# Pooled attention: normalizing by a diagonal in the transposing product, a byte activation for the first weights, paced staging

## The chip, the core and the metric

One core of one Trainium2 chip runs the whole program. The metric is the device time of one execution, in microseconds (us). Five engines work from queues of their own: TensorE (PE, with its weight loads as PEld), VectorE (DVE), ScalarE (ACT), GpSimd (POOL) and SyncE (SP), which here only issues transfers (DMA).

## The reference

Attention over 4 batches, 8 heads, 576 tokens of width 64, once over sequences pooled by 4 and once local (a band of 3 to each side), the two added; then two feed-forward nets over the 2304 tokens of width 512.

```python
def sm_attn(qq, kk, vv):
    s = scale * np.matmul(qq, kk.transpose(0, 1, 3, 2))
    s = s - np.max(s, axis=-1, keepdims=True)
    a = np.exp(s)
    a = a / (np.sum(a, axis=-1, keepdims=True) + 1e-09)
    return np.matmul(a, vv)
q_d = q.reshape(B, H, Sd, factor, D).mean(axis=3)
...
out_up = np.repeat(sm_attn(q_d, k_d, v_d), factor, axis=2)
...
out_local = np.matmul(attn, v)          # softmax over |i - j| < factor
x = out_up + out_local                  # to 2304 x 512
x = (silu(x @ w_gate) * (x @ w_val)) @ w_out          # 512 -> 1536 -> 512
return np.maximum(x @ w_in, 0.0) ** 2 @ w_out2        # 512 -> 2048 -> 512
```

## The kernel before, in words

A planner in the kernel (class Order) writes every engine's queue in advance: each piece of work is a Task, a chain of Stages, each with an engine, a cost and a function that emits instructions. At every step the planner takes the engine that can start first, and on it the ready stage with the lowest due time; products of the nets (flag `products`) go by a counter of their own and have preference on DVE and ACT. A task may not begin before its due time less its lead. On the chip each engine then works strictly in the order written.

The program has these stretches. (1) Attention, up to about 230 us, with the first net's product B1 beside it: 6 of the 12 feature blocks (NF = 6), each 12 matmuls for a gate and 12 for a value per tile of tokens (L945 to L947). While nothing else is there, up to about 30 us, PE is fed with products of zeros (L1058). (2) B, from about 230 us: the other 6 blocks, by a scheme with seven products in place of eight, over sums of blocks of weights and tokens. (3) D, from about 415 us: the first net's output product. (4) C, from about 565 us, and the last product: the second net.

Pooled attention works in 32 half-pieces, 8 per batch: one of two head rows, two (head pair, query half) combinations each, of 72 queries by 144 keys. One half-piece is: scores on PE (L690), their maximum (DVE L449, L451), two exponentials with their row sums on ACT (L462), the sum guarded and inverted on DVE (L475, L480), the weights scaled by it on DVE (`norm`, L484, 72x288), four 72x72 transposes on PE against `ident` (L709), a copy from PSUM on ACT (L715), the product with the values on PE (L728) and copies to `g` on ACT (L745).

Weights are 32-bit floats stored in 64-bit words of another number format, and are decoded: ACT rescales the upper word (L269), then either DVE alone shifts and merges three times (L278, L288, L288), or ACT makes the last bits from one byte (L275) and DVE merges twice (L288, L288). The first variant serves the 12 half-blocks of B1 (`w_task`, W_ACT = False), which then are split in a high and a low part (ACT L321, DVE L324). The second serves the weights of the later stretches, which `stage_task` decodes early and writes to DRAM (`w_sp`, L1140); `pair_task` reads them back, makes the sums of blocks and splits them (L1121, L1234).

All staged weights were due at 499 with a lead that let the gate and value blocks begin at 130 in the planner's time; the rest (down, in, out) had no due time, so that they filled whatever was free.

Of the kernel before, what the change touches and what calls it, by code (L numbers as in the profile page):

```python
# [9 lines left out]
F32 = mybir.dt.float32  # L10
# [4 lines left out]
AF = mybir.ActivationFunctionType  # L15
# [23 lines left out]
N_ATT, N_Y, N_GV, N_P, N_PT, N_V, N_XT, N_WST, N_WF, N_XH, N_SG, N_HH = 4, 2, 2, 5, 2, 2, 2, 3, 3, 2, 2, 2  # L39
N_QK = 3  # L40
NF = 6
W_ACT = False
ACT_BITS = (0, 1, 2, 3, 4)
NW1 = NF
EPS = 1e-9
# [20 lines left out]
def attn_moe_kernel(ctx: ExitStack, tc: tile.TileContext, qT, kT, vw, vin, vp, qp, kp, qs, ks, vs, maskc, masks, identc, wB, wC, out):  # L66
# [20 lines left out]
    def dve(n, fast=False):  # L87
        return 0.067 + n / (1920 if fast else 960)

    def act(n, psum=False):  # L90
        return (0.051 if psum else 0.093) + n / 1200
# [4 lines left out]
    def dma(size):  # L96
        return size / RATE
# [1 line left out]
    AFTER = {"v": 0.15, "a": 0.2, "p": 0.2, "t": 0.25}  # L99
    ATT_MAX, LOOK_V, LOOK_A, LOOK_P, LOOK_T, LOOK_D, PE_MARGIN = 2.0, 0.1, 0.0, 0.2, 0.05, 0.6, 0.1  # L100
    TICK, FILL_END, BUSY = 10.24 / 3, 40.0, 3180
    STAGE_AT, W_DUE0, W_STEP, X_DUE0, X_STEP, X_STEP0 = 130.0, 17.0, 2.2, 12.0, 20.0, 14.0
    CUT_T, CUT_J, W_LAG, Q_LATE, MASK_PE = 2, 4, 65.0, 10.0, 2
    V_LATE, V_LATE1, V_LATE0, V_LEAD, W_LEAD, LEAD, LATE = -15.0, -10.0, -5.0, 1000.0, 1000.0, 80.0, 500.0
    R_AT, R_STEP, LOC_LEAD, PIECE_LEAD, S_DVE, O_DVE = 3, 0.0, 60.0, 30.0, 1, 2
    SLACK, FIRST, EARLY, RATE, ISSUE, FLIGHT, AHEAD, ACC = 3.5, 24.0, 3.0, 70e3, 0.5, 1.7, 4.0, 1.0
# [16 lines left out]
    def after(ts):  # L123

        return max([0.0] + [t.ready for t in ts]) if all(t.done for t in ts) else None
# [310 lines left out]
    def softmax_stages(u, n, rows, width, source, scale, times, by_row, give, cond=None):  # L436

        size = n * width

        def biggest():
            if "p" not in u:
                u["p"] = p_tile(rows, n, width)
            u["mx"], u["sm"], u["rc"] = (
                att.tile([128, 8], F32, tag=tag, bufs=N_P + 1, name=tag)[:rows, :n] for tag in ("mx", "sm", "rc")
            )
            nc.vector.tensor_reduce(out=u["mx"], in_=u[source], op=ALU.max, axis=AX.X, negate=True)  # L449
            if by_row:  # L450
                nc.vector.tensor_scalar(out=u["mx"], in0=u["mx"], scalar1=scale, scalar2=None, op0=ALU.mult)  # L451

        def less():
            m = u["mx"].unsqueeze(2).to_broadcast([rows, n, width])
            nc.vector.tensor_tensor(out=u["p"], in0=u[source], in1=m, op=ALU.add)

        def exp():
            nc.scalar.activation(out=u["p"], in_=u["p"], func=AF.Exp, scale=scale)

        def exps():  # L460
            for c in range(n):
                nc.scalar.activation(  # L462
                    out=u["p"][:, c],
                    in_=u[source][:, c],
                    func=AF.Exp,
                    bias=u["mx"][:, c : c + 1],
                    scale=scale,
                    accum_out=u["sm"][:, c : c + 1],
                )

        def total():
            nc.vector.tensor_reduce(out=u["sm"], in_=u["p"], op=ALU.add, axis=AX.X)

# [12 lines left out]
        if by_row:
            first = [
                Stage("v", dve(size) + 0.2, biggest, cond=cond),
                Stage("a", n * (act(width, True) + 0.186), exps, (), give),
            ]  # L490
        else:
            first = [
                Stage("v", dve(size), biggest),
                Stage("v", dve(size), less, (), give),
                Stage("a", act(size), exp),
                Stage("v", dve(size), total),
            ]
        return first + [
            Stage("v", 0.07, guard),
            Stage("v", 0.09, one_over),  # L500
            Stage("v", dve(size), norm),
        ]

    def p_tile(rows, n, width):
        p = att.tile([128, 512], F32, tag="p", bufs=N_P, name="p")
# [195 lines left out]
    def global_task(b, h2, u, ins, due, combos):  # L701
        n = len(combos)

        def trans():
            u["ps"] = bank("att")
            for ci in range(n):
                for kc in range(2):
                    c = (ci * 2 + kc) * QC
                    nc.tensor.transpose(  # L709
                        u["ps"][:QC, c : c + QC], u["p"][:, ci, kc * QC : kc * QC + QC], ident[:QC, :QC]  # L710
                    )

        def turned():
# [409 lines left out]
    def bits(u, src, by_act=False):  # L1123

        def load():
            u["st"] = com.tile([128, 512, 2], I32, tag="wst", bufs=N_WST, name="wst")
            nc.sync.dma_start(out=u["st"], in_=src)

        return [Stage("d", dma(128 * 1024), load, ("wst",)), *decode(u, by_act)]

    staged, c_w, last_in = {}, {}, []

    def source(kind, f):
        return wC[f][:, kind] if kind in (IN, OUT) else wB[f if kind == DOWN else NF + f][:, kind - GATE]

    def stage_task(kind, f, start=0.0):
        u = {}

        def store():
            nc.sync.dma_start(out=w_sp[:, W_AT[kind] + f], in_=u["f"].bitcast(F32))  # L1140

        stages = [*bits(u, source(kind, f), kind in ACT_BITS), Stage("d", dma(128 * 512), store, (), ("wf",))]
        if kind == OUT and f >= NF2 // 2:
            stages[0].cond = lambda: after(last_in[min((f - NF2 // 2) // 2, NPC - 1) :][:1]) if len(last_in) == NPC else None
        staged[kind, f] = Task(stages, *((499.0, False, (), 499.0 - start) if start else (LATE,)))
        queues["w"].append(staged[kind, f])

    halves = {}
# [152 lines left out]
    def put(pairs):  # L1301
        for ins, both in pairs[:1]:
            queues["u"] += ins
        for i, (_, both) in enumerate(pairs):
            queues["u"] += [*(pairs[i + 1][0] if pairs[i + 1 :] else []), both]

    def unit(key, slot, *begin):
        put([pair_task(*key, slot, lambda *_: begin, begin=begin)])

    for q in range(NU // 2):  # L1310
        for kind in (GATE, VAL):
            for i in range(2):
                stage_task(kind, 2 * q + i, STAGE_AT)
    for f in range(NF1):
        stage_task(DOWN, f)
    for f in range(2 * NPC):
        stage_task(IN, f)
    for f in range(NF2):
        stage_task(OUT, f)
    unit(UNITS["B"][0], "wa", *v_sums)  # L1320
    for k in range(1, 5):
        unit(UNITS["B"][k], "wl", late_)
    for key in UNITS["B"][5:] + UNITS["D"][:2]:
        put([pair_task(*key, "wr", lambda *_: [late_b1_], begin=[late_])])


    ring, hc, rooms, free_rooms = [], {}, [], []
# [350 lines left out]
    for p in range(2, NPF):  # L1678
        was = p - 2

        def conds(b0, b1, was=was):
            return used("B", 0, was, in_blocks(GATE, b0, b1))

        down_units.append(pair_task(DOWN, p, "", conds, UNITS["B"][was], k=was, begin=[steps["B", 0, 1, 1, 0]]))
    put(down_units)


# [697 lines left out]
```

## Time and profile before

| | us |
|---|---|
| median of 3 runs | 919.73 |
| lowest and highest run | 917.60, 921.75 |
| time of the profiled execution | 917.94 |
| its span in the trace | 916.2 |
| PE, DVE, ACT busy in the span | 897.1, 764.3, 556.2 |

The time of an execution holds the span and some 1.7 us around it. Busy time is the time in which an engine had an instruction under way; a matmul's end is modelled, so that a busy PE may still hold pauses shorter than its pipeline. Idle time of PE is the first thing to look for, and beside it the granted clock, which is 1.00 at 2.4 GHz and 0.50 at 1.2 GHz.

### The profile page before, as it was taken

Reading aid. Unit: us, or ns where it says so; the run is one execution under the profiler, and the core shown is the slowest. Engines: PE = TensorE matmul, PEld = TensorE weight load, DVE = VectorE, ACT = ScalarE, POOL = GpSimd, SP = SyncE. Lnnn points to the kernel's source line nnn. Section 1 sums busy time; section 2 is a strip of 40 time slices with the busy share of each in tenths; the row PEclk is TensorE's granted clock in tenths of the full one; section 3 lists DMA queues with packets and bytes.
Section 4 is the critical chain, followed back from the end, with each engine's and each line's share of the span. In section 5 each row is a group of like instructions: output and inputs, shape, how many; then the busy total and the mean of one; then the engine's idle time right before and its main releaser. Section 6 shows DMA issues by size and latency. Waiting matters only on the chain.

```text
span 916.2 us, 18958 instructions
## 1 busy us (share of the span) xinstructions
PE 897.1 (98%) x7266; PEld 871.1 (95%) x7266; DVE 764.3 (83%) x1441; ACT 556.2 (61%) x1166; POOL 23.9 (3%) x31
## 2 busy tenths in 40 slices
PE   8989999999999999999999999999999999999998
PEld 7867989999999999999999999999999989999998
DVE  6999669698778997789989998998988797677774
ACT  3666364564546763564776668999987944444442
POOL 0201102000000000000000000000000000000000
PEclk9998999999999999999999999999999999999999
DMA  8999859656867674158767746888886653333411
GB/s 278 267 297 214 207 128 255 186 150 188 292 194 219 219 252 138 46 190 282 223 233 262 249 124 214 262 274 242 268 243 208 212 188 134 116 116 125 162 61 47
DMA packets 130615, 182.42 MB, mean 199 GB/s; under 512 B 24541, under 2 KB 98269, under 8 KB 129501
## 3 DMA queue, kind: packets, MB, share of 16 engines
q1 hardware_dynamic: 127068, 173.25, 59.6%
q0 software_dynamic: 3456, 7.96, 5.0%
q8 instruction: 57, 0.93, 0.4%
q14 instruction: 34, 0.27, 0.1%
HBM read 121.41 MB, written 59.77 MB: 198 GB/s over the span
## 4 chain that ended last, share of the span: by engine, by line
PE 79%; DVE 13%; ACT 3%; DMA 3%; issue 2%; SPq 0%; DVEq 0%; ACTq 0%
PE att L2192 10%; PE att L1471 10%; PE att L1833 6%; PE y L2192 6%; PE y L1566 4%; PE att L1566 4%; PE gv L1471 4%; PE y L1471 3%; PE gv L945 3%; PE gv L2192 3%; PE y L945 3%; PE gv L947 3%; PE gv L946 3%; PE y L1833 3%; PE y L946 2%; PE y L947 2%
## 5 line engine op out<-in xcount | busy, mean ns | idle before, releaser
L1121 DVE TENSOR_TENSOR xh<-xt,xh 128x768 fp32r<-128x768 f32 (+2 forms) x100 | 89.7, 899 | 26.0 <-ACT xh L2130 16.1
L945 PE MATMUL gv<-xh,w 128*128 128x256 f32 (+1 forms) x216 | 66.4, 308 | 0.0
L947 PE MATMUL gv<-xh,w 128*128 128x256 f32 (+1 forms) x216 | 63.8, 295 | 0.7 <-DVE w L324 0.7
L946 PE MATMUL gv<-xh,w 128*128 128x256 f32 (+1 forms) x216 | 63.5, 294 | 0.0
L2192 PE MATMUL att<-wl,xh 128*128 128x256 f32 x408 | 57.7, 283 | 2.2 <-ACT xh L2130 1.3
L1471 PE MATMUL att<-xh,wl 128*128 128x384 f32 x288 | 54.7, 336 | 1.5 <-DVE xh L1121 1.4
L2192 PEld LDWEIGHTS att<-wl,xh 128*128 128x128 f32 x408 | 52.8, 191 | 2.6 <-ACT xh L2130 1.5
L288 DVE SCALAR_TENSOR_TENSOR wf<-wst,wf 128x512 int32<-128x512 int32 x80 | 54.4, 684 | 0.5
L2208 ACT ACTIVATE os<-att 128x256 f32<-128x256 f32 x36 | 13.7, 384 | 66.8 <-PE att L2192 66.8
L1471 PEld LDWEIGHTS att<-xh,wl 128*128 128x128 f32 x288 | 50.4, 188 | 2.2 <-DVE xh L1121 2.1
L945 PE MATMUL y<-xh,w 128*128 128x256 f32 (+1 forms) x168 | 52.0, 309 | 0.0
L946 PE MATMUL y<-xh,w 128*128 128x256 f32 (+1 forms) x168 | 49.7, 296 | 0.0
L947 PE MATMUL y<-xh,w 128*128 128x256 f32 (+1 forms) x168 | 49.7, 296 | 0.0
L970 ACT ACTIVATE sg<-gv 128x256 f32<-128x256 f32 (+1 forms) x48 | 19.7, 410 | 49.4 <-PE gv L947 49.2
L269 ACT ACTIVATE wf<-wst 128x512 f32<-128x512 f32 x68 | 45.6, 671 | 0.3 <-DMA wst<-wB 0.2
L1566 PE MATMUL y<-xh,wl 128*128 128x384 f32 x216 | 42.2, 336 | 0.4 <-DVE hl L1121 0.2
L945 PEld LDWEIGHTS gv<-xh,w 128*128 128x128 f32 x216 | 41.0, 190 | 1.6 <-issue 0.4
L2192 PE MATMUL att<-wr,xh 128*128 128x256 f32 x306 | 42.3, 282 | 0.0
L947 PEld LDWEIGHTS gv<-xh,w 128*128 128x128 f32 x216 | 41.0, 190 | 1.2 <-DVE w L324 1.1
L1566 PE MATMUL att<-xh,wl 128*128 128x384 f32 x216 | 41.5, 335 | 0.0
L946 PEld LDWEIGHTS gv<-xh,w 128*128 128x128 f32 x216 | 41.1, 190 | 0.0
L288 DVE SCALAR_TENSOR_TENSOR wf<-wf,wst 128x512 int32<-128x512 int32 x56 | 38.0, 683 | 3.5 <-ACT wst L275 3.2
(285 smaller groups left out, 2564.8 us busy)
## 6 DMA issues: line engine op xcount, KB each, us to landing
wst<-wB SPq DMA_DIRECT2D x36, 512.0 KB, 4.3
wst<-wC SPq DMA_DIRECT2D x32, 512.0 KB, 5.5
w_sp<-wf SPq DMA_DIRECT2D x48, 256.0 KB, 3.0
h_sp<-hr SPq DMA_DIRECT2D x62, 192.0 KB, 2.8
wst<-w_sp SPq DMA_DIRECT2D x22, 512.0 KB, 4.7
h_sp<-hl SPq DMA_DIRECT2D x58, 192.0 KB, 2.6
xt<-y_sp SPq DMA_DIRECT2D x21, 384.0 KB, 4.0
hr<-h_sp SPq DMA_DIRECT2D x4, 1536.0 KB, 6.0
```

The lines of the kernel that those rows point to most:

```text
L269: nc.scalar.activation(out=u["f"].bitcast(F32), in_=u["st"][:, :, 1].bitcast(F32), func=AF.Abs, scale=2.0**-112)
L288: nc.vector.scalar_tensor_tensor(out=u["f"], in0=in0, scalar=by, in1=in1, op0=op, op1=ALU.bitwise_or)
L945: nc.tensor.matmul(ps[:, :n], w[:, 0], xh[:, 0, kk, :n], start=(kk == 0), stop=False)
L946: nc.tensor.matmul(ps[:, :n], w[:, 0], xh[:, 1, kk, :n], start=False, stop=False)
L947: nc.tensor.matmul(ps[:, :n], w[:, 1], xh[:, 0, kk, :n], start=False, stop=(kk == KD - 1))
L970: nc.scalar.activation(out=u["s"], in_=u["g"][:, :n], func=AF.Tanh, scale=0.5)
L1121: nc.vector.tensor_tensor(out=out, in0=a, in1=b, op=op)
L1471: nc.tensor.matmul(ps, w[:, a, c], x[:, b, kk], start=P in (1, 5) and kk == 0 and i == 0, stop=P in (2, 3, 4) and kk == 1 and i == 2, skip ...
L1566: nc.tensor.matmul(ps, w[:, a, c], x[:, b, kk], start=P in (1, 5) and kk == 0 and i == 0, stop=P in (2, 3, 4) and kk == 1 and i == 2, skip ...
L1833: nc.tensor.matmul(banks[a_banks][d][:, :T2], w[:, a, 128 * d : 128 * d + 128], x[:, b, q], start=fresh and q == 0 and m == 0, stop=final ...
L2192: nc.tensor.matmul(ps, hl[a][:, p], w[:, b], start=tag is not None and p == 0 and i == 0, stop=(P in (2, 3, 4) or (split and P == 7)) and ...
L2208: nc.scalar.activation(out=at(c), in_=banks[q, own][:, :256], func=AF.Copy)
```

## The change

Three edits, and the planner then writes all queues anew.

1. The pooled softmax is no longer scaled by DVE. ACT makes, for each of the two combinations, a 72x72 tile `id`, the identity with its rows scaled by the inverted sums, and PE multiplies by it where it transposed.
2. The 12 first half-blocks of weights are decoded by the second variant (W_ACT = True).
3. Staged gate and value blocks are due one by one, at 150 and every 9 after, and may begin 30 before that; down blocks begin only behind the pairs of B that are three places ahead, and the pairs of D wait for the last of them.

```diff
-W_ACT = False
+W_ACT = True
...
-    STAGE_AT, W_DUE0, W_STEP, X_DUE0, X_STEP, X_STEP0 = 130.0, 17.0, 2.2, 12.0, 20.0, 14.0
-    CUT_T, CUT_J, W_LAG, Q_LATE, MASK_PE = 2, 4, 65.0, 10.0, 2
+    STAGE_STEP, STAGE_LEAD, STAGE_AT, W_DUE0, W_STEP, X_DUE0, X_STEP, X_STEP0 = 9.0, 30.0, 150.0, 17.0, 2.2, 12.0, 20.0, 14.0
+    CUT_T, Q_LATE, MASK_PE = 2, 10.0, 2
+    D_BEHIND = 3
...
-            Stage("v", dve(size), norm),
-        ]
+        def scaled():
+            u["id"] = att.tile([128, 2 * QC], F32, tag="id", bufs=N_P, name="id")[:rows].rearrange("p (c q) -> p c q", q=QC)
+            for c in range(n):
+                nc.scalar.activation(
+                    out=u["id"][:, c], in_=ident[:rows, :rows], func=AF.Copy, scale=u["rc"][:, c : c + 1]
+                )
+
+        last = Stage("a", n * act(rows), scaled) if by_row else Stage("v", dve(size), norm)
+        return first + [Stage("v", 0.07, guard), Stage("v", 0.09, one_over), last]
...
-                    nc.tensor.transpose(
-                        u["ps"][:QC, c : c + QC], u["p"][:, ci, kc * QC : kc * QC + QC], ident[:QC, :QC]
+                    nc.tensor.matmul(
+                        u["ps"][:QC, c : c + QC],
+                        u["p"][:, ci, kc * QC : kc * QC + QC],
+                        u["id"][:, ci],
+                        start=True,
+                        stop=True,
                     )
...
+        if kind == DOWN:
+            stages[0].cond = lambda: after(last_b[min(f // 2 + D_BEHIND, NU - 1) :][:1])
-        staged[kind, f] = Task(stages, *((499.0, False, (), 499.0 - start) if start else (LATE,)))
+        staged[kind, f] = Task(stages, *((start, False, (), STAGE_LEAD) if start else (LATE,)))
...
-                stage_task(kind, 2 * q + i, STAGE_AT)
+        stage_task(kind, 2 * q + i, STAGE_AT + STAGE_STEP * n)
...
-        down_units.append(pair_task(DOWN, p, "", conds, UNITS["B"][was], k=was, begin=[steps["B", 0, 1, 1, 0]]))
+        down_units.append(pair_task(DOWN, p, "", conds, UNITS["B"][was], k=was, begin=[steps["B", 0, 1, 1, 0], staged[DOWN, NF1 - 1]]))
```

What it does to the queues is seen at three places. The lines of the changed kernel are a few higher (L475 is L476 there). First DVE, about 58 us, where batch 1's pooled softmax stands among the first weights (`sm` and `rc` are sums and their inverses, `wf` a weight being decoded, `w_...` its low part, `hh` a net's result). Before:

```order
L475 TENSOR_SCALAR sm<-sm 72x2 x2
L480 RECIPROCAL rc<-sm 72x2 x2
L324 TENSOR_TENSOR w_568<-wf,w_568 128x512
L278 TENSOR_SCALAR wf<-wf 128x512
L484 TENSOR_TENSOR p<-p,rc 72x288
L288 SCALAR_TENSOR_TENSOR wf<-wst,wf 128x512
```

Now:

```order
L993 SCALAR_TENSOR_TENSOR hh<-sg,gv 128x256
L325 TENSOR_TENSOR w_717<-wf,w_717 128x512
L476 TENSOR_SCALAR sm<-sm 72x2
L450 TENSOR_REDUCE mx<-att 72x2
L452 TENSOR_SCALAR mx<-mx 72x2
L481 RECIPROCAL rc<-sm 72x2
```

The scaling (L484) and the shift of `wf` (L278) are gone from DVE; the inverse (L481) is now its last work for a half-piece.

Second ACT, at the same place of the program (`p,sm` exponentials, `pt` the copy of a transposed tile). Before:

```order
L462 ACTIVATE p,sm<-att,mx 72x144 x4
L321 ACTIVATE w_568<-wf 128x512
L269 ACTIVATE wf<-wst 128x512
L715 ACTIVATE pt<-att 72x288
L321 ACTIVATE w_830<-wf 128x512
L462 ACTIVATE p,sm<-att,mx 72x144 x2
```

Now:

```order
L502 ACTIVATE id<-ident,rc 72x72 x2
L463 ACTIVATE p,sm<-att,mx 72x144 x4
L979 ACTIVATE sg<-gv 128x256
L593 ACTIVATE pt<-att 128x512
L724 ACTIVATE pt<-att 72x288
L502 ACTIVATE id<-ident,rc 72x72 x6
```

The diagonals stand on ACT between the exponentials and the copies, and they wait there for DVE's inverses.

Third DVE where D begins, between two low parts `xh` of its first tiles (`ws` and `wl` are sums and low parts of a pair of staged weights, `hl` a partial result). Before:

```order
L1121 TENSOR_TENSOR xh<-xt,xh 128x768
L288 SCALAR_TENSOR_TENSOR wf<-wf,wst 128x512
L1121 TENSOR_TENSOR hl<-y,hl 128x384
L288 SCALAR_TENSOR_TENSOR wf<-wst,wf 128x512
L1614 SCALAR_TENSOR_TENSOR hl<-hl 128x384
L288 SCALAR_TENSOR_TENSOR wf<-wf,wst 128x512
L1121 TENSOR_TENSOR xh<-hl,xh 128x768
```

Now:

```order
L1130 TENSOR_TENSOR xh<-xt,xh 128x768
L1130 TENSOR_TENSOR ws<-wst,ws 128x256
L289 SCALAR_TENSOR_TENSOR wf<-wf,wst 128x512
L1130 TENSOR_TENSOR hl<-y,hl 128x384
L1130 TENSOR_TENSOR wl<-wst,wl 128x512
L1626 SCALAR_TENSOR_TENSOR hl<-hl 128x384
L1130 TENSOR_TENSOR wl<-wst,wl 128x512
L1130 TENSOR_TENSOR wl<-ws,wl 128x768
L1130 TENSOR_TENSOR xh<-hl,xh 128x768
```

Two merges of staged weights have left this gap, and four steps of a pair of weights have come in. On PE the order holds 93 products of zeros in place of 98, and 128 products with `id` in place of 128 transposes.

## Rows read from the trace of the kernel before

**Rows 1.** The page: busy time by engine; the chain's shares.

```profile
PE 897.1 (98%) x7266; PEld 871.1 (95%) x7266; DVE 764.3 (83%) x1441; ACT 556.2 (61%) x1166; POOL 23.9 (3%) x31
PE 79%; DVE 13%; ACT 3%; DMA 3%; issue 2%; SPq 0%; DVEq 0%; ACTq 0%
```

**Rows 2.** Windows: length, busy per engine, PE clock, DMA share, GB/s.

```profile
0.00:28.00 28.00, 25.02 (x295) 20.36 (x296) 19.71 (x55) 12.65 (x39) 2.12 (x6) 1.00 0.93 277
28.00:51.00 23.00, 23.00 (x366) 20.92 (x365) 22.18 (x59) 14.49 (x47) 6.15 (x7) 1.00 1.02 273
51.00:71.00 20.00, 15.79 (x194) 12.72 (x192) 18.56 (x56) 13.87 (x47) 0.84 (x1) 0.83 0.93 279
71.00:96.00 25.00, 22.81 (x324) 19.88 (x320) 23.48 (x62) 14.02 (x38) 5.25 (x6) 0.93 0.94 216
98.00:140.00 42.00, 42.00 (x513) 38.71 (x513) 26.22 (x79) 19.11 (x72) 5.49 (x7) 1.00 0.68 168
140.00:230.00 90.00, 90.00 (x1219) 84.32 (x1215) 77.69 (x205) 47.56 (x127) 3.47 (x4) 1.00 0.70 192
230.00:290.00 60.00, 59.97 (x354) 59.65 (x354) 48.48 (x86) 30.05 (x52) 0.00 (x0) 1.00 0.72 231
```

**Rows 3.** PE's waits up to 230 us: us in total, times, longest.

```profile
PE att L580 <- DVE p L484: 2.1, 1, 2.1
PE att L728 <- ACT pt L715: 1.7, 2, 1.2
PE att L709 <- ACT g L745: 0.8, 2, 0.6
PE gv L947 <- DVE w L324: 0.7, 2, 0.4
PE att L538 <- ACT g L745: 0.6, 1, 0.6
PE att L601 <- ACT pt L588: 0.5, 1, 0.5
```

**Rows 4.** Groups of instructions: busy us, mean ns | idle before.

```profile
L484 DVE TENSOR_TENSOR p<-p,rc 72x288 f32<-72x288 f32 x32 | 14.3, 449 | 0.2
L278 DVE TENSOR_SCALAR wf<-wf 128x512 int32<-128x512 int32 x12 | 5.0, 422 | 0.2 <-ACT wf L269 0.2
L745 ACT ACTIVATE g<-att 64x72 f32<-64x72 f32 x64 | 14.4, 225 | 13.4 <-PE att L728 12.8
L275 ACT ACTIVATE wst<-wst 128x512 int32<-128x512 uint8 x56 | 37.7, 673 | 0.0
L709 PE MATMUL att<-ident,p 72*72 72x72 f32 x128 | 13.7, 234 | 0.8 <-ACT g L745 0.8
L728 PE MATMUL att<-pt,vd 72*64 72x72 f32 x256 | 14.2, 240 | 1.7 <-ACT pt L715 1.7
```

**Rows 5.** DVE's timeline, about 58 us: start, us.

```profile
58.98 0.45 DVE L484 TENSOR_TENSOR p<-p,rc 72x288 f32<-72x288 f32 x1
59.35 0.68 DVE L288 SCALAR_TENSOR_TENSOR wf<-wst,wf 128x512 int32<-128x512 int32 x1
```

**Rows 6.** PE's timeline, about 40 us: transposes, products, and what starts next.

```profile
39.98 0.66 PE L709 MATMUL att<-ident,p 72*72 72x72 f32 x8
40.44 0.36 PE L945 MATMUL gv<-xh,w 128*128 128x256 f32 x1
42.04 0.72 PE L728 MATMUL att<-pt,vd 72*64 72x72 f32 x16
42.69 0.39 PE L538 MATMUL att<-mask_b,ident_b 128*128 128x512 bf16 x1
44.09 0.69 PE L709 MATMUL att<-ident,p 72*72 72x72 f32 x8
44.62 0.38 PE L538 MATMUL att<-mask_b,ident_b 128*128 128x256 bf16 x2
```

**Rows 7.** Windows of L709 alone: length, PE busy, PEld busy, clock, DMA.

```profile
0.00:28.00 28.00, 1.72 (x16) 1.10 (x16) 1.00 0.93 277
28.00:98.00 70.00, 5.09 (x48) 3.61 (x48) 0.93 0.97 254
98.00:230.00 132.00, 6.87 (x64) 4.44 (x64) 1.00 0.70 185
```

**Rows 8.** PE's timeline: products of zeros, and the next; the start of D.

```profile
18.97 1.04 PE L1058 MATMUL y<-zeros 128*128 128x256 bf16 x8
19.84 0.42 PE L580 MATMUL att<-ident,xh 128*128 128x128 f32 x2
422.26 2.01 PE L1833 MATMUL att<-xh,wl 128*128 128x384 f32 x10 [1.18 <-DVE xh L1121]
```

**Rows 9.** DVE's timeline as D begins.

```profile
417.65 0.95 DVE L1121 TENSOR_TENSOR xh<-xt,xh 128x768 fp32r<-128x768 f32 x1
418.52 0.68 DVE L288 SCALAR_TENSOR_TENSOR wf<-wf,wst 128x512 int32<-128x512 int32 x1
419.12 0.55 DVE L1121 TENSOR_TENSOR hl<-y,hl 128x384 f32<-128x384 f32 x1
421.26 0.95 DVE L1121 TENSOR_TENSOR xh<-hl,xh 128x768 fp32r<-128x768 f32 x1
```

More of the change, by code (lines that the diff above doesn't have):

```diff
@@ L497, in softmax_stages @@
             ]
-        return first + [
-            Stage("v", 0.07, guard),
-            Stage("v", 0.09, one_over),
-            Stage("v", dve(size), norm),
-        ]
+        def scaled():
[6 more added lines that the diff above has]
+        return first + [Stage("v", 0.07, guard), Stage("v", 0.09, one_over), last]
     def p_tile(rows, n, width):
@@ L1129, in bits @@
         return [Stage("d", dma(128 * 1024), load, ("wst",)), *decode(u, by_act)]
-    staged, c_w, last_in = {}, {}, []
+    staged, c_w, last_in, last_b = {}, {}, [], []
     def source(kind, f):
@@ L1143, in stage_task @@
         if kind == OUT and f >= NF2 // 2:
-            stages[0].cond = lambda: after(last_in[min((f - NF2 // 2) // 2, NPC - 1) :][:1]) if len(last_in) == NPC else None
-        staged[kind, f] = Task(stages, *((499.0, False, (), 499.0 - start) if start else (LATE,)))
+            stages[0].cond = lambda: after(last_in[min((f - NF2 // 2) // 2, NPC - 1) :][:1])
+        if kind == DOWN:
+            stages[0].cond = lambda: after(last_b[min(f // 2 + D_BEHIND, NU - 1) :][:1])
+        staged[kind, f] = Task(stages, *((start, False, (), STAGE_LEAD) if start else (LATE,)))
         queues["w"].append(staged[kind, f])
@@ L1305, in put, with unit @@
             queues["u"] += [*(pairs[i + 1][0] if pairs[i + 1 :] else []), both]
[L1307 to L1312, printed above, removed]
-                stage_task(kind, 2 * q + i, STAGE_AT)
+    def unit(key, slot, conds, begin):
+        pair = pair_task(*key, slot, lambda *_: conds, begin=begin)
+        last_b.append(pair[1])
+        put([pair])
+    for n, (q, kind, i) in enumerate((q, kind, i) for q in range(NU // 2) for kind in (GATE, VAL) for i in range(2)):
+        stage_task(kind, 2 * q + i, STAGE_AT + STAGE_STEP * n)
     for f in range(NF1):
@@ L1319, in attn_moe_kernel @@
         stage_task(OUT, f)
-    unit(UNITS["B"][0], "wa", *v_sums)
+    unit(UNITS["B"][0], "wa", v_sums, v_sums)
     for k in range(1, 5):
-        unit(UNITS["B"][k], "wl", late_)
+        unit(UNITS["B"][k], "wl", [late_], [late_])
     for key in UNITS["B"][5:] + UNITS["D"][:2]:
-        put([pair_task(*key, "wr", lambda *_: [late_b1_], begin=[late_])])
+        unit(key, "wr", [late_b1_], [late_])
     ring, hc, rooms, free_rooms = [], {}, [], []
```

## The prediction

> **What bounds the kernel now.** I read the page's busy times and chain first. PE is busy 897.1 of 916.2 us and holds 79% of the chain that ended last; DVE holds 13%, ACT 3% [rows 1]. So a change on DVE or ACT is worth only what it takes out of PE's idle or slow time, and what it adds to PE counts at once. Second, the windows, to see where PE has such time. The reader is to compare PE's busy time with the window's length: from 98 to 290 us nothing is missing but 0.03 us, and before that two windows miss 20.00 - 15.79 = 4.2 us and 25.00 - 22.81 = 2.2 us, together 6.4, between 51 and 96 us [rows 2]. Those two alone also show a granted clock under 1: 0.83 and 0.93. Between 1.2 and 2.4 GHz that is 2 x 0.17 x 20 + 2 x 0.07 x 25 = 10.3 us at the lower level. Half of that is work lost, 5.1 us, less what fell into idle time (the 1.2 us wait for `pt`, [rows 3]): 4.5. So this stretch loses 6.4 + 4.5 = 10.9 us. That is all that attention can give back. DVE is its fullest engine: 18.56 of 20 and 23.48 of 25 us; ACT has 13.87 and 14.02 [rows 2]. Third, who ended PE's waits: DVE's scaling and low parts of weights 2.1 + 0.7, ACT's copies 1.7 + 0.8 + 0.6 + 0.5 [rows 3]. ACT's copies sit in chains from PE over ACT to PE, in which PE has nothing else because weights and tiles, DVE's work, are late; I read DVE as the root there, but that is a reading.
>
> A measurement of this kernel can tell about 0.5%, 4.6 us, from no change.
>
> **DVE's relief.** 32 scalings at 449 ns and 12 shifts at 422 ns leave DVE [rows 4]: 14.4 + 5.1 us over the program. What counts lies between 28 and 98 us: 48 of the 128 transposes stand there [rows 7], four to a half-piece, so 12 scalings, 5.4 us; and about 10 of the 12 shifts, 4.2 us (the first two stand before). In a full queue an instruction costs less than its duration: the scaling at 58.98 is followed by a start at 59.35, 0.37 us later, 0.82 of its 0.45 [rows 5]. So 0.82 x 9.6 = 7.9 us. I take all of it as recovered, of the 10.9 lost: **-7.9**.
>
> **ACT's load.** 64 diagonals and 12 byte activations come in. The trace has no 72x72 activation scaled per row; the nearest is the 64x72 copy to `g`, 225 ns, and the byte activation itself is there at 673 ns [rows 4]: 14.4 + 8.1 us on an engine busy 556 of 916. In the fullest window, 51 to 71 us, four half-pieces (8 x 0.225 = 1.8) and some four weights (2.7) make 13.87 into 18.4 of 20 [rows 2]. That still fits: **0**. If it does not, see the second rival.
>
> **PE's price of the diagonal.** A transpose leaves one record per product: 32 half-pieces x 4 = 128, and L709 counts 128. The product with the values is an fp32 matmul of equally many products, 32 x 4, and counts 256 [rows 4]: two records each. So 128 transposes become 256 loads and products. What a record costs is read from starts: eight transposes from 39.98 to the next start at 40.44 take 58 ns each, eight from 44.09 to 44.62 take 66. Sixteen records of L728 from 42.04 to 42.69 take 41 ns each [rows 6], but these go to alternating halves of the output's partitions, which the new product, with all 72 in one, does not. I take 58 ns for each added record; below, 2 x 41 - 58 = 24 ns; above, 2 x 66 - 58 = 74. Placed by [rows 7]: 16 before 28 us, 48 from 28 to 98, 64 after.
> - Before 28 us PE is fed with zeros, and 5 products of zeros fewer stand there now: 16 x 58 ns = 0.9, less 5 x 0.109 (eight take 18.97 to 19.84, [rows 8]): **+0.4**.
> - From 28 to 98: 48 x 58 ns = 2.8. 10.9 - 7.9 = 3.0 us of loss is left, which this work can partly fill; I take half as hidden: **+1.4**.
> - After 98: 64 x 58 ns = 3.7, with no idle time on PE to hide them [rows 2]: **+3.7**.
>
> A rule speaks against the change: the Trainium skill (TensorE: Matmul & The Clock Gate, section Terms) has the transpose mode four times faster for FP32 than the plain product. The record counts of this trace show two, not four, and no row shows a full-width fp32 product alone. By that rule the sum would be some 15 us higher; it is the third rival.
>
> **Due times.** The staged blocks' DVE merges move within stretches where PE waits for nothing: DVE has 48.48 of 60 us in B's first part [rows 2], so their move there is worth **0**; SP and POOL get no new transfer, only another order of the same. The place where it can cost is the start of D. There PE waited 1.18 us for a low part `xh` [rows 8] that ran at 421.26, 3.6 us behind the one at 417.65, with three merges (0.60 each by their starts), two half-tile sums (0.47) and the 0.87 of `xh` itself between [rows 9]. Now one merge is left and four steps of a pair come in: one of 256 columns (about 0.34, half a merge's columns), two of 512 (0.60, as a merge) and one of 768 (0.87, as `xh`). That is -1.2 + 2.4 = **+1.2** if DVE is full there, and 0 if not; I take 1.2, since its rows stand without a gap.
>
> **Sum.** -7.9 + 0.4 + 1.4 + 3.7 + 1.2 = -1.2 us. The profiled execution took 917.94 (span 916.2 and 1.7 around), so 916.7; the median of the runs shown, 919.73, is 1.8 above it, and with that the forecast is **918.5**: no change that can be measured. Its own range runs from 915 to 924 by the ends of the recovery and of D.
>
> **The rivals.**
> 1. *Faster: the stretch clears wholly and the diagonal is cheap.* All 10.9 us come back, the added records cost 24 ns (112 x 24 ns = 2.7 from 28 us on), the first 28 us even out (16 x 24 ns - 0.5 = -0.1), D costs nothing: -8.3, so 911.4. With 58 ns a record it is still -10.9 + 0.4 + 2.8 + 3.7 = -4.0, 915.7. For it: DVE is the fullest engine exactly where PE loses. Against: four of the six waits are ended by ACT. It decides above 4.6 us gained, which needs nearly the whole loss back and a price below some 50 ns. Chance 0.25.
> 2. *Slower: ACT takes DVE's place.* 3.6 of the 6.4 us of waits were ended by ACT. Each half-piece now needs its two diagonals (0.45) and a PE part longer by 4 x 58 ns, against the scaling's 0.37 gone: 0.3 us more on its chain. If PE keeps waiting on those chains, only DVE's 2.8 us come back, and 12 chains lengthen by 0.3, 3.7 us: -2.8 + 0.4 + 2.8 + 3.7 + 3.7 + 1.2 = +9.0, 928.7. It decides where ACT's fullest window passes some 19 of 20 us. Against: 18.4 by the sum above. Chance 0.10.
> 3. *Slower: an fp32 product streams four times.* Then every product costs 3 x 58 = 174 ns more in place of 58, 116 x 112 = 13.0 us from 28 us on and 1.9 before: 918.5 + 14.9 = 933.4. Against: two records for each fp32 product in L728, of 240 ns each as the transpose's 234 [rows 4]. Chance 0.04.
> 4. *The due times move nothing that matters:* then D's +1.2 falls away and 917.3 is left, inside the forecast's case.
>
> **How the numbers follow.** The forecast's case has 0.61, the rivals 0.25, 0.10 and 0.04. Against 919.73 the bound lies at 915.1 and 924.3: faster 0.25, no change 0.61, slower 0.14. The range runs from 911.5, which leaves out the far end of the first rival (about 0.08), to 926.5, which leaves out most of the second and the third (about 0.1).
>
> **What would show it.** The records of the product with `id` should number 256, and the eight of a half-piece take some 0.46 us where its four transposes took 0.23. In 51 to 96 us PE's idle time should fall from 6.4 to under 3 us, the clock's mean rise towards 1.00, and ACT stay below 19 of 20 us. From 98 us to the end of attention PE should be full and about 4 us longer in the same work. The wait at the start of D should be 1 to 2.5 us. I am wrong if PE's records stay at 128 or cost under 30 ns, if the idle time of the stretch stays, or if a wait of more than 2 us appears where PE was full.

## The result, and the profile after

The changed kernel takes 927.71 us (median of 6 runs, 926.98 to 928.84), the kernel before 917.88 in the same comparison (6 runs, 916.98 to 921.75): a ratio of 1.010, 95% interval 1.0081 to 1.012. It is slower by 9.2 us (7.4 to 11.0); forecast was no change, 918.5, and the range ended at 926.5. Where "us slower" stands below without more, it is a ratio less 1, times 918.

The page of the changed kernel, busy time by engine and the chain's shares:

```profile
PE 907.8 (98%) x7389; PEld 883.4 (95%) x7389; DVE 749.9 (81%) x1397; ACT 576.9 (62%) x1242; POOL 23.8 (3%) x31
PE 85%; DVE 7%; ACT 5%; DMA 2%; issue 1%; SPq 0%; ACTq 0%; DVEq 0%
```

Against [rows 1]: DVE's busy time fell by 14.4 us and its share of the chain from 13% to 7%, as the change intends. (The groups that left it are 14.3 + 5.0 us [rows 4]; an instruction starts before its neighbour ends [rows 5], so that less goes from the busy time.) PE took 10.7 us more, and the span grew by 9.9, from 916.2 to 926.1. PE's idle time hardly changed over the whole (19.1 before, 18.3 after).

The windows of the changed kernel (length, busy of PE, PEld, DVE, ACT and POOL, PE clock, DMA share, GB/s):

```profile
51.00:71.00 20.00, 16.48 (x214) 13.41 (x213) 15.83 (x50) 16.84 (x61) 0.56 (x1) 0.92 0.86 281
71.00:96.00 25.00, 23.91 (x318) 20.91 (x317) 20.13 (x45) 17.99 (x51) 7.25 (x9) 0.86 1.04 230
98.00:140.00 42.00, 42.00 (x498) 39.65 (x496) 22.68 (x70) 20.52 (x75) 1.70 (x2) 1.00 0.53 142
```

Against [rows 2]: between 51 and 96 us DVE is relieved (18.56 to 15.83, 23.48 to 20.13), ACT stays under 19 of 20 us (16.84), and still PE misses 3.5 and 1.1 us, 4.6 in place of 6.4. The clock is no better: 0.92 and 0.86 are 2 x 0.08 x 20 + 2 x 0.14 x 25 = 10.2 us at 1.2 GHz, where it had been 10.3.

PE's waits of the changed kernel up to 240 us, the largest behind one of 2.3 us for the zeros, which both kernels have (us in total, times, longest):

```profile
PE att L606 <- ACT p L463: 1.2, 1, 1.2
PE att L695 <- ACT g L754: 0.9, 1, 0.9
PE att L737 <- ACT pt L724: 0.7, 1, 0.7
PE att L695 <- ACT pt L593: 0.7, 1, 0.7
```

In [rows 3] DVE ended 2.8 of 6.4 us; now ACT ends every one of these. The product with `id` (L714, the transpose L709 before), alone: its windows (length, PE busy, PEld busy, clock, DMA, GB/s), its group, and the group of the diagonals.

```profile
0.00:28.00 28.00, 2.90 (x32) 2.43 (x32) 1.00 0.91 272
28.00:98.00 70.00, 9.47 (x96) 8.48 (x96) 0.93 0.98 257
98.00:235.00 137.00, 10.87 (x128) 9.57 (x128) 1.00 0.67 185
```

```profile
L714 PE MATMUL att<-id,p 72*72 72x72 f32 x256 | 23.2, 239 | 0.2 <-ACT g L754 0.2
L502 ACT ACTIVATE id<-ident,rc 72x72 f32<-72x72 f32 x64 | 17.8, 354 | 0.1
```

There are 256 records in place of 128, each as long as one had been (239 and 234 ns). Busy PE time goes from 1.72 + 5.09 + 6.87 = 13.7 us [rows 7] to 23.2.

Where the 9.9 us arise is read from the same instructions in both timelines, those behind PE's waits. Of the changed kernel (start, us; the wait in brackets):

```profile
400.43 1.31 PE L1578 MATMUL att<-xh,wa 128*128 128x384 f32 x6 [1.30 <-ACT hr L1603]
429.75 1.65 PE L1845 MATMUL att<-xh,wl 128*128 128x384 f32 x4 [2.42 <-DVE xh L1130]
573.73 0.97 PE L1483 MATMUL att<-xh,wl 128*128 128x384 f32 x4 [1.68 <-DVE xh L1130]
747.75 0.50 PE L2204 MATMUL att<-wl,xh 128*128 128x256 f32 x2 [1.34 <-ACT xh L2142]
```

and of the kernel before (that of D is in [rows 8]):

```profile
393.94 1.31 PE L1566 MATMUL att<-xh,wa 128*128 128x384 f32 x6 [0.67 <-ACT hr L1591]
565.33 0.96 PE L1471 MATMUL att<-xh,wl 128*128 128x384 f32 x4 [1.45 <-DVE xh L1121]
739.34 0.50 PE L2192 MATMUL att<-wl,xh 128*128 128x256 f32 x2 [1.34 <-ACT xh L2130]
```

| up to | lag, us | new in this part |
|---|---|---|
| the wait in B, without it | 5.9 | attention and B's first part |
| that wait | 6.5 | +0.6: 1.30 for 0.67 |
| start of D | 7.5 | +1.0: its wait is 2.42 for 1.18 |
| start of the second net | 8.4 | +0.9: lower clock behind that wait; 0.2 of it the wait of 1.68 for 1.45 |
| last product | 8.4 | 0 |
| end | 9.9 | +1.5: lower clock behind the waits there |

The lower clock in the last lines, from windows of the changed kernel around the two places:

```profile
426.00:434.00 8.00, 5.58 (x24) 5.26 (x23) 8.00 (x11) 3.40 (x7) 0.00 (x0) 0.79 0.75 260
746.00:754.00 8.00, 5.83 (x34) 5.42 (x33) 6.45 (x14) 3.86 (x7) 0.00 (x0) 0.79 0.26 109
```

and of the kernel before around the same waits:

```profile
738.00:746.00 8.00, 5.83 (x46) 5.63 (x47) 7.64 (x17) 4.79 (x8) 0.00 (x0) 1.00 0.21 85
420.00:428.00 8.00, 6.82 (x40) 6.50 (x39) 8.00 (x12) 3.00 (x5) 0.00 (x0) 1.00 0.95 320
```

At 746 us PE is busy as long as before (5.83) but does 34 products where it did 46: 2 x 0.21 x 8 = 3.4 us at 1.2 GHz, 1.7 of work lost.

The 5.9 us of the first line, by PE's records from its first to its first product of B (from each start to the next, idle and half of the time at the lower clock taken out): the records against `ident` or `id` go from 9.2 to 18.4, +9.2; idle time 7.1 to 4.9, -2.2; time lost to the clock is 5.1 in both; the zeros (93 for 98) and all else together -0.4. That makes 6.6, with 12 products of the first net counted in that stand behind B's first product now. The first part of B has 0.7 less.

### The profile page after: what moved, and what is told of

Read it like the earlier page. It is cut to its first block, busy times and chain, and to the rows that moved or that the text cites. A ratio compares the mean times of both kernels' runs of the same rounds, so it can differ in the third digit from the quotient of the medians.

```text
span 926.1 us, 19258 instructions
## 1 busy us (share of the span) xinstructions
PE 907.8 (98%) x7389; PEld 883.4 (95%) x7389; DVE 749.9 (81%) x1397; ACT 576.9 (62%) x1242; POOL 23.8 (3%) x31
## 4 chain that ended last, share of the span: by engine, by line
PE 85%; DVE 7%; ACT 5%; DMA 2%; issue 1%; SPq 0%; ACTq 0%; DVEq 0%
PE att L2204 10%; PE att L1483 10%; PE att L1845 7%; PE y L2204 6%; PE y L1578 5%; PE att L1578 5%; PE gv L1483 3%; PE gv L954 3%; PE y L1483 3%; PE gv L955 3%; PE gv L956 3%; PE gv L2204 3%; PE y L1845 3%; PE y L954 3%; PE y L955 2%; PE y L956 2%
## 5 line engine op out<-in xcount | busy, mean ns | idle before, releaser
L289 DVE SCALAR_TENSOR_TENSOR wf<-wf,wst 128x512 int32<-128x512 int32 x68 | 46.5, 684 | 12.7 <-ACT wst L276 12.2
L2220 ACT ACTIVATE os<-att 128x256 f32<-128x256 f32 x36 | 13.7, 384 | 67.9 <-PE att L2204 67.9
L289 DVE SCALAR_TENSOR_TENSOR wf<-wst,wf 128x512 int32<-128x512 int32 x68 | 46.6, 685 | 0.5
L276 ACT ACTIVATE wst<-wst 128x512 int32<-128x512 uint8 x68 | 45.6, 671 | 0.1
L954 PEld LDWEIGHTS gv<-xh,w 128*128 128x128 f32 x216 | 41.2, 191 | 2.2 <-ACT w L322 0.5
L956 PEld LDWEIGHTS gv<-xh,w 128*128 128x128 f32 x216 | 41.2, 191 | 0.3 <-DVE w L325 0.3
```

What stands on the lines that cost most here:

```text
L276: nc.scalar.activation(out=u["st"][:, :, 0], in_=byte, func=AF.Copy, scale=1 / 32, bias=-15.5 / 32)
L289: nc.vector.scalar_tensor_tensor(out=u["f"], in0=in0, scalar=by, in1=in1, op0=op, op1=ALU.bitwise_or)
L954: nc.tensor.matmul(ps[:, :n], w[:, 0], xh[:, 0, kk, :n], start=(kk == 0), stop=False)
L956: nc.tensor.matmul(ps[:, :n], w[:, 1], xh[:, 0, kk, :n], start=False, stop=(kk == KD - 1))
```

## The experiments

Theories. **P**: the loss is PE's price of the second record of each product. **A**: it is the diagonal's way over ACT. Of the staging: the due times, or the order as a whole, make the losses in B and at D. Of the idle time that did not come back: DVE is its root (the forecast), or not, or only where it stands in the chain to a wait (**Place**).

| kernel | median, us | before beside it | ratio, 95% |
|---|---|---|---|
| e1_plain | 926.46 | 918.12 | 1.0090 (1.0066 to 1.0113) |
| e2_actscale | 923.92 | 918.12 | 1.0061 (1.0039 to 1.0083) |
| e3_diag | 939.43 | 918.12 | 1.0229 (1.0204 to 1.0254) |
| e4_nodiag | 924.12 | 918.12 | 1.0059 (1.0039 to 1.0080) |
| e5_wact | 928.41 | 919.67 | 1.0085 (1.0068 to 1.0103) |
| e6_due | 922.74 | 919.67 | 1.0028 (1.0009 to 1.0046) |
| e8_nonorm | 917.85 | 919.67 | 0.9980 (0.9964 to 0.9997) |
| e9_after_again | 927.43 | 919.67 | 1.0074 (1.0054 to 1.0095) |
| e12_fp32r | 922.46 | 918.43 | 1.0033 (1.0017 to 1.0050) |
| e7_nodue | 931.57 | 918.43 | 1.0136 (1.0115 to 1.0157) |
| e10_pool | 925.02 | 918.43 | 1.0063 (1.0044 to 1.0083) |
| e11_price | 928.61 | 918.43 | 1.0102 (1.0083 to 1.0121) |
| e13_two_local | 919.11 | 918.42 | 0.9997 (0.9975 to 1.0019) |
| e14_both | 919.76 | 918.42 | 1.0005 (0.9985 to 1.0025) |

### PE's price: e1, e2, e12

e1_plain, on the kernel before:

```diff
-                    nc.tensor.transpose(
-                        u["ps"][:QC, c : c + QC], u["p"][:, ci, kc * QC : kc * QC + QC], ident[:QC, :QC]
-                    )
+                    nc.tensor.matmul(
+                        u["ps"][:QC, c : c + QC],
+                        u["p"][:, ci, kc * QC : kc * QC + QC],
+                        ident[:QC, :QC],
+                        start=True,
+                        stop=True,
+                    )
```

> The kernel before with its queues word for word as they were; only the 128 transposes of the pooled softmax are plain fp32 products against the same identity, so PE has 256 records there. Theory P (the loss is PE's price of the second record, 80 ns for each added one, the spacing of the records in the changed kernel): 10.3 us more on PE, of which the idle time before 98 us hides 2 to 3: 925 to 928 against 917.9. Theory A (the loss is the diagonal's way over ACT, and a record costs the 24 to 58 ns of the forecast): 920 to 923.

Measured: 8.3 us slower (6.1 to 10.4), in P's range. Windows of its L709 alone, columns as above:

```profile
0.00:28.00 28.00, 2.90 (x32) 2.43 (x32) 1.00 0.95 277
28.00:98.00 70.00, 8.50 (x96) 7.35 (x96) 0.93 0.93 247
98.00:235.00 137.00, 11.55 (x128) 9.50 (x128) 1.00 0.67 178
```

With no other instruction moved, 128 more records make PE's busy time for them 23.0 us in place of 13.7, and the span 7.2 longer (923.4). From start to start the records take 18.5 us where the transposes took 9.2, so an added one costs 73 ns, not the 80 expected. Some of it fell into idle time, though DVE does all of its work here:

```profile
28.00:98.00 70.00, 64.95 (x924) 57.18 (x924) 65.15 (x175) 43.12 (x131) 12.50 (x14) 0.93 0.93 247
```

PE's idle time is 5.05 us there, and 6.40 in the kernel before (its window is shown with e8). The waits at D and after stand as before. This one edit loses nearly as much as the whole change.

e2_actscale, on the changed kernel (the planner's costs, and so its queues, stay):

```diff
-                    out=u["id"][:, c], in_=ident[:rows, :rows], func=AF.Copy, scale=u["rc"][:, c : c + 1]
+                    out=u["p"][:, c], in_=u["p"][:, c], func=AF.Copy, scale=u["rc"][:, c : c + 1]
...
-                        u["id"][:, ci],
+                        ident[:QC, :QC],
```

with `transpose` in the place of the product.

> The changed kernel with its queues as they are; ACT scales the two weights tiles by their rows (72x144) where it made the two diagonals, and PE transposes with the identity, one record a product. DVE is relieved as in the change, ACT's chain is as long or a little longer. Theory P: the 10.3 us of PE fall away: 916.5 to 920. Theory A: the chain over ACT stays, so 925 to 929.

e12_fp32r, on the changed kernel:

```diff
-                    out=u["p"][:, c],
+                    out=u["p"][:, c].bitcast(F32R),
...
-                    out=u["id"][:, c], in_=ident[:rows, :rows],
+                    out=u["id"][:, c].bitcast(F32R), in_=ident[:rows, :rows],
...
-                        u["p"][:, ci, kc * QC : kc * QC + QC],
-                        u["id"][:, ci],
+                        u["p"][:, ci, kc * QC : kc * QC + QC].bitcast(F32R),
+                        u["id"][:, ci].bitcast(F32R),
```

> The changed kernel with its queues as they are; the weights and the diagonal are written and read as fp32r (fewer bits), which should leave one record a product, 128 in place of 256. ACT makes the same diagonals, DVE is relieved as in the change. Theory P (PE's price): the 9.4 us that the added records take in the changed kernel's attention come off, less what turns into waits: 918 to 922.5, the waits at the start of D as in the change. If the chains over ACT fill what PE gives back, as in the kernel with ACT's scaling (923.9): 923 to 926.

Measured: 5.6 us slower than before (e2) and 3.0 (e12), that is 3.6 and 6.2 less than the change's 9.2. e2 fell between its two theories; e12 is P's, at the upper end of its range. Of e12, the product's group:

```profile
L714 PE MATMUL att<-id,p 72*72 72x72 f32 x128 | 13.9, 241 | 1.5 <-ACT g L754 1.3 <-DVE sm L476 0.2
```

One record a product, as long as one of the two had been. But not all that PE gives back is gained. The window of attention's crowded part, of the changed kernel and of e12:

```profile
28.00:98.00 70.00, 65.37 (x921) 57.21 (x921) 58.26 (x151) 54.09 (x168) 13.81 (x16) 0.93 0.98 257
```

```profile
28.00:98.00 70.00, 64.90 (x846) 55.63 (x844) 56.67 (x148) 54.03 (x169) 13.89 (x16) 0.88 0.92 243
```

e12 has 75 records fewer there, and PE is nearly as busy. Its idle time up to 235 us (windows from 0, 28 and 98 us) is 9.9 us where the changed kernel has 7.2. So P holds for the price, and theory A for a remainder: with less to do, PE waits longer for the same chains. The clock's mean, 0.88 for 0.93 (16.8 us at 1.2 GHz for 9.8), is not shown to be e12's own: this profile is of a run of 924.46 us with a clock of 0.989 over the whole execution, where the median of e12's eleven is 922.46 us and 0.991. The ten runs of the changed kernel have 0.991 to 0.994.

### The edits one by one: e3 to e7, e9, e11

e3_diag is the first edit alone, e5_wact the second (`W_ACT = True`), e6_due the third; e4_nodiag is the change without the first, e7_nodue without the third. Their diffs are the parts of the change's. e9_after_again is the changed kernel once more.

> The kernel before with the diagonal alone (first edit); weights and due times as before. Theory P: 924 to 928, that is nearly the whole loss of the change. If the due times and the start of D made half of the loss (wait 1.2 longer, clock lower twice): 920 to 923.

> The changed kernel without the diagonal (DVE scales as before, PE transposes): byte activations and due times alone. Theory P: 916 to 920, no difference from before that can be told. If the due times and the start of D made half of the loss: 921 to 924, with the wait of 2.4 us at the start of D.

> The kernel before with the byte activations alone (second edit): DVE loses the 12 shifts of the first weights, ACT takes 12 byte activations. If the losses in B and at the start of D that the change without its diagonal showed (3.3 and 3.3 us) come from the due times: 915 to 918.5 here, no such loss. If they come from an order of the planner that any edit may tip: 920 to 925, with waits in B or D.

> The kernel before with the due times alone (third edit). If the due times make the losses in B and at the start of D: 920 to 924.5, attention as before. If the losses need the second edit's order too: 916 to 919.

> The changed kernel with the staging rules of before (first and second edit alone). Each edit alone lost its time in the first pairs of B (waits of 5 to 8 us there, with either the diagonal or the byte activations). If the due times mend that: 932 to 945 here, with such waits between 285 and 310 us. If they do not matter in the full change: 926 to 929, or 1 to 2 less for the start of D.

> The changed kernel once more, for a second profile: the times again 926.5 to 929. If the lower clock at the start of the last product (1.5 us there, beside the same waits as before) belongs to the kernel, it stands there again for 3.4 us; if it is chance, the clock is 1.00 there and the profiled execution some 1.5 us shorter. The one behind the wait at the start of D should stand in both.

The table shows that the edits do not add up: alone they cost 21.0, 7.8 and 2.6 us, together 9.2. e3 and e5 came out slower than either theory had them. e4 (5.4 us) is at the second one's end, but not by the wait it names (0.58 at D): PE waited 3.0 us in B and 3.6 in five pieces for `xh` in D. e6 is in its first range, e7 just under its first, with the waits that it names, and e9 in its own. What e3, e5 and e7 have in common is a place: B's first pairs. PE's waits of e3 from 285 to 310 us, then of e7 in the same stretch:

```profile
PE gv L1574 <- ACT wr L1242: 3.1, 1, 3.1
PE gv L1574 <- ACT wl L1242: 2.1, 1, 2.1
PE gv L1574 <- DVE wl L1129: 2.0, 1, 2.0
```

```profile
PE gv L1574 <- DVE wr L1129: 1.6, 1, 1.6
PE gv L1574 <- ACT wr L1242: 1.4, 1, 1.4
```

`wl` and `wr` are the split sums of the staged weights' first pairs; with the old staging they come late once either of the first two edits stands (5.0 us of such waits in e5), and the clock falls behind these waits (0.80 from 285 to 320 us in e3, 0.86 from 285 to 310 in e7). The changed kernel and e6 have no wait there, e4 one of 0.2 us. So the due times mend what the other two edits break in B (e7 is 12.5 us slower, the change 9.2), and they pay elsewhere. e6, PE's timeline behind the waits in B and at D:

```profile
394.42 0.79 PE L1570 MATMUL att<-xh,wa 128*128 128x384 f32 x3 [1.33 <-ACT hr L1595]
423.74 0.96 PE L1837 MATMUL att<-xh,wl 128*128 128x384 f32 x4 [2.42 <-DVE xh L1122]
```

They are the changed kernel's to 0.03 us, and e7, without the third edit, has 0.68 and 1.23 there. The longer wait in B is the due times': it is 1.30 to 1.83 us in every kernel with the third edit and at most 0.81 in every one without it. The one at D is not theirs alone. e3, which has the old due times, has it too, and e4, with the new ones, has 0.58 there and other waits behind it. Of e3:

```profile
443.64 2.18 PE L1841 MATMUL att<-xh,wl 128*128 128x384 f32 x11 [2.42 <-DVE xh L1129]
```

The lower clock behind these waits is not as sure. In e6 the window from 420 to 428 us, with the same wait, shows 1.00, and so does the last product:

```profile
420.00:428.00 8.00, 5.58 (x32) 5.25 (x31) 8.00 (x12) 4.02 (x7) 0.00 (x0) 1.00 0.74 263
739.00:747.00 8.00, 5.83 (x46) 5.42 (x46) 7.63 (x16) 4.79 (x8) 0.00 (x0) 1.00 0.27 112
```

This is one run of e6, of 919.43 us and a clock of 0.994 over the whole execution; the median of its twelve is 922.74 us and 0.989, so that others lost clock that this profile does not show. e9, the second profile of the changed kernel (ratio 1.0074, so its loss came out as 6.8 us), has 0.80 and 0.79 at the two places, as the first.

e11_price tells the planner what the product costs:

```diff
-                Stage("t", 0.12 * n, trans, ("att", "pt"), ("p",), share=0.54),
+                Stage("t", 0.3 * n, trans, ("att", "pt"), ("p",), share=0.54),
```

> The changed kernel with one number of the planner changed: a half-piece's products with the diagonal cost 0.6 us in its plan in place of 0.24, as they do on the chip. PE's work is the same. If a part of the loss is a plan that runs ahead of PE (11.5 us over the 32 half-pieces): 922 to 926, by fewer waits in attention and at the start of D. If PE's price is all of it: 926 to 929; another order may also lose some us in B or D.

Measured: 9.4 us slower, no better than the change. That the plan runs ahead of PE is not the loss, or another order lost as much again: PE waited 5.1 us for `pt` between 28 and 98 us there.

### Why the idle time stayed: e8, e10, e13, e14

e8_nonorm, on the kernel before:

```diff
         def norm():
+            if by_row:
+                return
```

> The kernel before with its queues as they are, but without DVE's 32 scalings (the pooled softmax is left unnormalized): DVE relieved by 14.4 us, nothing added to ACT or PE. Theory D (the forecast: DVE is the root of the idle time and the lower clock in 51 to 96 us): 12 scalings x 0.37 = 4.4 us come back there, idle time under 3.5 us, 913 to 914.5. Theory A (the chains over ACT and the order itself hold PE there): under 2 us come back, 916 to 918.5.

Measured: 1.8 us faster (0.3 to 3.3), in theory A's range, with 14.4 us of DVE's work gone and nothing added anywhere. Its window of the crowded part, and the place of PE's longest wait:

```profile
28.00:98.00 70.00, 63.52 (x913) 55.65 (x911) 63.26 (x169) 43.59 (x133) 11.29 (x13) 0.93 0.95 253
```

```profile
52.80 1.94 PE L582 MATMUL att<-ident,p 128*128 128x128 f32 x8 [2.08 <-DVE p L486]
```

The same of the kernel before:

```profile
28.00:98.00 70.00, 63.60 (x910) 55.43 (x909) 66.18 (x181) 43.41 (x134) 12.82 (x15) 0.93 0.97 254
```

```profile
53.53 1.69 PE L580 MATMUL att<-ident,p 128*128 128x128 f32 x8 [2.08 <-DVE p L484]
```

PE's idle time there is 6.5 us where it was 6.4, the clock is the same, and the wait of 2.08 us is there to the hundredth. With that the forecast's reading falls. The wait belongs to a local tile: DVE sums, inverts and scales two tiles of 128x512 for it in one run, and in the kernel before none of the pooled scalings stands on DVE between 40.60 and 58.98 us [rows 5]:

```profile
40.60 0.45 DVE L484 TENSOR_TENSOR p<-p,rc 72x288 f32<-72x288 f32 x1
52.69 1.29 DVE L484 TENSOR_TENSOR p<-p,rc 128x512 f32<-128x512 f32 x2
```

What DVE saves elsewhere it spends in waits: 3.5 us of them from 20 to 98 us before, 5.9 in e8, most for ACT, which waits for DVE and PE in its turn. So the new theory was Place, and it takes away just the two scalings ahead of that wait (two local tiles stay unnormalized):

```diff
         def norm():
+            if not by_row:
+                scaled_local.append(1)
+                if len(scaled_local) in (5, 6):
+                    return
```

e14_both returns in the other case as well.

> The kernel before with its queues as they are, but without the two scalings of local attention (128x512, 1.29 us together) that stand on DVE just ahead of PE's longest wait at 51 to 54 us (those two tiles are left unnormalized). Theory Place (DVE's work counts only in the chain to a wait): that wait falls from 2.08 to some 0.8 us, and 1 to 2.5 us come back, as much as or more than without all 32 pooled scalings: 915.5 to 917.5. Theory None (DVE's work is not what PE waits for): the wait stays at 2 us, 917.5 to 919.

> The same without those two scalings and without all 32 pooled scalings (all left unnormalized): 15.7 us of DVE taken away. Theory Place: the two gains add up, the first wait at 0.8 us, the waits for ACT's copies as before, 914.5 to 917. The forecast's reading (all of DVE's relief in the stretch comes back): 911 to 913.5. Theory None: as without the pooled scalings alone, 916.5 to 918.5.

Of e13, the place of that wait:

```profile
52.75 0.63 PE L586 MATMUL att<-ident,p 128*128 128x128 f32 x4 [0.45 <-DVE sm L477]
```

The windows of the crowded part, of e13 and of e14:

```profile
28.00:98.00 70.00, 64.49 (x928) 56.11 (x925) 66.52 (x182) 45.25 (x137) 12.18 (x14) 0.95 0.96 257
```

```profile
28.00:98.00 70.00, 64.98 (x905) 56.52 (x903) 61.98 (x166) 43.45 (x132) 13.36 (x16) 0.90 0.98 261
```

1.3 us of DVE's work in the right place took 1.6 us off the wait, where 14.4 us beside it took off nothing. So Place holds for the wait. It does not show in the time: 0.9997 and 1.0005 tell no gain, and the medians lie above Place's ranges and above None's (919.11 and 919.76, with 918.42 for the kernel before beside them). In e14 one sees where the gain went: PE's idle time is down to 5.0 us, but its clock is 0.90, 14.0 us at 1.2 GHz where 0.93 makes 9.8. Its twelve runs bear this out: the median of their clocks over the whole execution is 0.991, and 0.994 for the 23 of the kernel before. Why the clock fell is not shown. The waits for ACT's copies (1.7 us for `pt`, 0.6 to 0.8 for one of `g`) stand in e8, e13 and e14 as before. e13's profile had the higher clock, 0.95, and a span of 915.1; its 12 runs lie between 916.1 and 922.3.

e10_pool gives the 32 scalings to POOL in the queues of before:

```diff
+        def norm_pool():
+            rc = u["rc"].unsqueeze(2).to_broadcast([rows, n, width])
+            nc.gpsimd.tensor_tensor(out=u["p"], in0=u["p"], in1=rc, op=ALU.mult)
+
+        last = Stage("v", dve(size), norm_pool) if by_row else Stage("v", dve(size), norm)
...
-            Stage("v", dve(size), norm),
```

> The kernel before with its queues as they are, but the 32 scalings run on POOL, which has room (24 of 916 us). Nothing is added to PE or ACT. By the run without scalings (915.6 span, 0.2 to 1.8 us gained): 916 to 919 if POOL's scaling takes no longer than DVE's queue did; 919 to 922 if it takes over 1 us each and the transposes wait for it.

Measured: 5.8 us slower, outside both. POOL took 822 ns for each scaling (DVE 449), and PE waited 2.3 us for the first of them, which stood in POOL's queue behind a transfer of `kd` that started only at 21.12 us. No variant that does all of the work was faster than the kernel before, so none is put forward.

## Why the prediction was wrong, step by step

**DVE's relief, -7.9: failed, and it is the largest error.** "I take all of it as recovered" was the step. Work off the fullest engine was taken as time off the stretch. In 28 to 98 us idle time fell by 1.8 us (6.4 to 4.6) and the clock stayed at 0.93. Even of these 1.8, e1 has 1.35 by its added records alone, with DVE not relieved at all. e8 shows that all 32 scalings are worth 1.8 us (3.3 at most, by the interval), where 12 of them had been put at 4.4 (the shifts' part of the 7.9, some 3.5, was not tested alone in unchanged queues); e13 shows that what stands in the chain to a wait shortens it; e14 that even this can be given back to the clock. "I read DVE as the root there, but that is a reading": the reading was wrong for the waits that ACT ended, and DVE's 2.1 us was ended by work that the change leaves alone.

**PE's price: the mechanism right, the size wrong.** 256 records were forecast and came. 58 ns for an added one was read from the cheaper of two runs of transposes side by side [rows 6]; over all 128, from start to start, it is (18.5 - 9.2) / 128 = 73 ns in e1, just under the upper bound of 74. The kernel before had it in its trace: 9.2 us for 128 transposes are 72 ns each. The eight records of one half-piece in the changed kernel:

```profile
40.41 0.68 PE L714 MATMUL att<-id,p 72*72 72x72 f32 x8
40.90 0.37 PE L954 MATMUL gv<-xh,w 128*128 128x256 f32 x1
```

61 ns each here, but over the 21 half-pieces that stand alone there it is 73 on the mean, 60 to 92. Half of 2.8 us was taken as hidden from 28 to 98 us, and that was about right: e1's idle time there is 1.35 lower. 5.5 us were counted, 6.0 with the zeros left in place as e1 leaves them, and e1's span grew by 7.2. The third rival was wrong as well: the Trainium skill (TensorE: Matmul & The Clock Gate, section Terms) gives the transpose mode a factor of four over the plain product for FP32, and here it is a factor of two, 256 records for 128 with the mean of one unchanged, 18.5 us for 9.2.

**ACT's load, 0: right by its bound, wrong in size.** ACT had 16.84 of 20 us, under the 18.4 forecast. But a diagonal takes 354 ns, not the 225 of the copy to `g`. The Trainium skill (ScalarE: Activation LUTs, section What ACT_TABLE_LOAD costs) would have had it: a fixed 186 ns, 0.833 a column, and some 93 for each operand that comes as a column of a tile, so an estimate of 339 for 72 columns with the scale so given. The trace's 354 is near it. No run took the diagonals alone away without changing PE or DVE, so what they cost is open.

**Due times.** At D the step was right: +1.2 forecast, 1.18 to 2.42 measured, and DVE's way from one `xh` to the next grew as it was added up, from 3.61 us [rows 9] to 4.81:

```profile
423.94 0.95 DVE L1130 TENSOR_TENSOR xh<-xt,xh 128x768 fp32r<-128x768 f32 x1
428.75 0.95 DVE L1130 TENSOR_TENSOR xh<-hl,xh 128x768 fp32r<-128x768 f32 x1
```

e6 and e7 would tie it to the third edit, but e3 has the same wait without that edit: it comes with an order of the planner that the diagonal alone can bring about too. "Worth 0" in B was wrong by 0.6: the wait for `hr` went from 0.67 to 1.30. That the third edit also prevents a loss in B was not seen.

**Not in the sum at all:** the clock behind later waits, some 0.7 us at D and 1.5 at the last product, in both profiles of the changed kernel. That it is the change's doing is not shown: see what stays open.

**The rivals.** The second gave 928.7, near the 927.7 measured, but not by its mechanism alone: it had ACT past 19 of 20 us, which did not happen, and 3.7 us of longer chains, which no run shows; that no more than DVE's 2.8 us would come back was right (idle time fell by 1.8, most of which e1 has without any relief), and PE's price made most of the rest. Its chance of 0.10 was too low, since it was tied to a full ACT where the waits already named ACT's chains. The fourth, due times that move nothing, fell with D's wait.

**What stays open:** why the clock falls behind the same two waits of 1.34 and 0.82 us at the last product in seven of the sixteen profiles (the changed kernel's two, e3, e5, e10, e12 and e14; e10 and e14 have the queues of before) and not in the others; why it fell behind the same wait of 2.42 us at D in three profiles (the changed kernel's two and e2) and not in e3, e6, e11 and e12; why the single losses, 8.3 us in e1 and 5.4 in e4, sum to more than the change's 9.2; and how much of the orders' losses in B is chance of the planner.

## What to carry to other kernels

Work taken from a busy engine is a gain only where it stands between the last thing a wait depended on and its end: list the instructions of that chain, and test the reading by leaving the work out with all queues unchanged, before anything is rewritten to remove it. Price a PE instruction by the mean over all of its records, from start to the next start, not by the best run of them, and count records: here an fp32 product left two where a transpose left one. Where a planner writes the queues, single edits do not add up: judge them in the order in which they will run, and look at the stages that the edit does not mention.

## What the runs showed of the hardware

- A product of fp32r operands leaves one record of 241 ns where the fp32 product leaves two of 239, and a transpose one of 234 [rows 4]. The kernel with it, otherwise the changed one, is 6.2 us less slow, by the two ratios.
- A 72x72 activation with its scale from a tile takes 354 ns, a 64x72 copy 225 [rows 4].
- The same scaling takes 822 ns on POOL and 449 on DVE.
- Less idle time on PE need not bring a higher clock: e14, with 5.0 us of it in 28 to 98 us where the kernel before has 6.4, has 0.90 there against 0.93.
- Behind equal waits the clock fell in some profiles and not in others (0.79 in the changed kernel, 1.00 in e6, both at D and at the last product), which costs some 1.5 us at the last product.
- One kernel's time goes with its granted clock: of 23 runs of the kernel before, beside e13 and e14, the six with 0.998 over the whole execution took 916.2 to 918.2 us, the four with 0.987 or 0.989 took 921.6 to 924.9.
